# Two more output buffers, an unchecked load of flags and three more branched ranks in a fused attention and mixture-of-experts kernel

## The chip, the cores and the metric

The kernel runs on one core of a Trainium2 chip. The metric is the device time of one execution in microseconds (us). The engines are named as the profile names them: PE is TensorE with its matmuls, PEld its loads of weights, DVE is VectorE, ACT is ScalarE, POOL is GpSimd and SP is SyncE, which here issues most of the transfers.

## The reference, cut to what matters

A clustered attention feeds a mixture of experts. Queries and keys of 4 batches, 8 heads and 768 positions are each assigned to one of 16 centroids, and a query sees only the keys of its own cluster. The result, 3072 rows of 512 numbers, is the input of the experts. Four groups of four experts make 16; every row goes to one expert, found by two argmax (group, then expert in the group), and its result is scaled by the product of the two softmax weights:

```python
for g in range(G):
    mask_g = g_idx == g
    xg = x[mask_g]
    ...
    for e in range(Eg):
        mask_e = e_idx == e
        h = np.maximum(xg[mask_e] @ w1[g, e], 0.0)
        ye = h @ w2[g, e]
        combined = g_w[mask_g][mask_e] * e_w[mask_e]
        out[tok_idx] = combined[:, None] * ye
```

Here `w1` of one expert is 512 x 1024 and `w2` 1024 x 512, in float32. The kernel computes each product in float16 with a high and a low part, so that one product becomes three: high by high, high by low and low by high.

## The kernel before, in words

The attention and the routing take the first 400 us or so. The experts follow, and the change lies there alone. The expert with most rows is treated first, in a part A and a part B that is woven into it (`bridge`). The other fifteen are sorted by their number of rows, and the sorted place is the rank. Rank k has a fixed capacity, `caps` at line 773: 288, 272, 256, 240, 232, 224, 216, 208, 200, 192, 184, 176, 168, 160 and 160 rows. One round of the loop in `ranks` holds the first product of rank k (`up`) and the second product of rank k - 1 (`down`), eight steps of each, taken in turn, and between them the next pieces of the stream of weights (`fill`): a load by SP, the high part by ACT or POOL (line 833 or 835), the low part by DVE (line 836).

The order of the instructions on PE, ACT and DVE is the order of the program (`manual_schedule` with PINNED, line 1511). An instruction that waits therefore holds all that stands behind it on its engine. POOL and SP are not pinned in that list, but work in the order of their queues as well.

`up` (line 1047) computes two of eight feature blocks at a time, each in a psum tile out of three. ACT takes the relu out of each into `hh` (line 1069) and DVE the low part into `hl` (line 1070); after that the psum tile is free again. `down` (line 1074) has two ways. Rank 2 goes by rows: the result is an output tile of up to 128 rows at once. The other ranks go by features (`feature_major`): four feature blocks of 24 products each, taken out by ACT and DVE into `yh` and `yl` (lines 1104 and 1105), and in the next round `settle` turns them back with PE into output tiles, at step 2.

`emit` (line 1160) finishes an output tile: ACT scales it by the weights of the rows into `y` (line 1163), a tile of 128 x 512 float32 out of three buffers, and POOL issues an indirect transfer that stores the rows where they belong (line 1164). A buffer can be written again when its store has landed.

Most ranks have fewer rows than their capacity. `widths` (line 1274) computes for all ranks at once whether the number of rows is no more than a narrower size, the capacity less an entry of `LESS` (16 for rank 9, 24 for ranks 10 and 11), and packs the answers as bits of one integer, `wi`. PE loads it into a register once, in step 5 of the second half of `bridge` (line 1457). The load has bounds, 0 and 2 to the 16th less one, and these are checked on PE at run time. `at_width` (line 1297) then writes a block of products twice, under an `If` and its `Else`, with the narrow or with the full number of columns; a block's first product, which starts the sum, is full in both. All blocks of `up` branch so, 12 products for each of two feature blocks. Those of `down` do for ranks under `CHOSEN`, 9 (line 761), in one group of 24 products; from rank 9 on a feature block is two groups of 12 products without a branch, one at an even and one at an odd step.

The tile `xTA` (line 940) has 4 x 2 x 256 float16 numbers on each partition. It holds the turned rows of part A and is read by the first products of part A.

Of the kernel before, what the change touches and what calls it, by code (L numbers as in the profile page):

```python
# [14 lines left out]
F32 = mybir.dt.float32  # L15
# [4 lines left out]
ET = mybir.EngineType  # L20
# [4 lines left out]
P = 128  # L25
# [720 lines left out]
class Experts:  # L746
# [11 lines left out]
    TURNED, TURN = (3, 4, 6, 14), 3  # L758
    HI = (0, 0, 0, 1, 0, 0, 0, 1)
    LEAD = 12  # L760
    CHOSEN, BOUND = 9, 15
    LESS = 16, 32, 32, 24, 24, 24, 24, 24, 24, 16, 24, 24, 24, 16, 24

    def __init__(self, ctx, tc, R, w1, w2, out, stage, wa):
# [137 lines left out]
    def fetch(self):  # L902

        nc, R, CA, KD = self.nc, self.R, self.CA, self.R.KD
        nt = -(-CA // P)
        sz = [min(P, CA - t * P) for t in range(nt)]
        tab = self.small("tabA", [P, nt, 2])
        tv = R.table.rearrange("(e s) w -> e s w", s=R.BS)[bass.ds(self.f0, 1)].rearrange("e s w -> (e s) w")
        self.nt = -(-max(self.caps) // P)
        self.tb = self.small("tb", [R.E, self.nt * P, 2])  # L910
        while R.done < R.B - 2:
            yield
        for _ in range(READ + 2):
            yield
        with self.after(), self.tc.issue_after(self.cfg["mr"].ins) if "mr" in self.cfg else ExitStack():
            for t, n in enumerate(sz):
                R.reads(nc.sync.dma_start(out=tab[0:n, t], in_=tv[t * P:t * P + n]))
            R.reads(nc.sync.dma_start(out=self.tb, in_=R.table.rearrange("(e s) w -> e s w", s=R.BS)[0:R.E, 0:self.nt * P]))
        for _ in range(READ):
            yield  # L920
        ids = self.small("idA", [P, nt], I32)
        g = self.small("gA", [P, nt])
        with self.after():
            for t, n in enumerate(sz):
                nc.vector.tensor_copy(out=ids[0:n, t:t + 1], in_=tab[0:n, t, 0:1])
                nc.vector.tensor_scalar(out=g[0:n, t:t + 1], in0=tab[0:n, t, 1:2], scalar1=1.0 / (XS * WS * WS), scalar2=None, op0=ALU.mult)
        self.colsA = [g[0:n, t:t + 1] for t, n in enumerate(sz)], [ids[0:n, t:t + 1] for t, n in enumerate(sz)]

        rows = R.N - R.N // R.B
        xgs = []  # L930
        for t, n in enumerate(sz):
            xf = self.cfg["ld"].tile([P, KD * P * 3 // 2], F32, name=("qx", "kx", "vx")[t])[:, 0:self.D]
            nc.vector.memset(xf, 0.0)
            xgs.append(xf.bitcast(F16).rearrange("p (k a x) -> p k a x", a=2, x=P))
            if rows:
                with self.tc.issue_after(self.cfg["los"][0].ins) if "los" in self.cfg else ExitStack():
                    self.gather(ids[0:n, t:t + 1], n, xgs[t], rows)
            for _ in range(2):
                yield
        xTA = self.wa.tile([P, KD, 2, CA], F16, name="xTA")  # L940
        self.xTA = xTA.rearrange("p k a m -> p a k m")
        for t, n in enumerate(sz):
            nc.sync.dma_start_transpose(out=xTA.rearrange("p k a m -> p (k a) m")[:, :, t * P:t * P + n], in_=xgs[t][0:n].rearrange("p k a x -> p (k a x)"))
            yield

    def open(self, ctx):
        tc = self.tc
        late = ctx.enter_context(tc.tile_pool(name="econst2", bufs=1))
        self.small = lambda name, shape, dt=F32: late.tile(shape, dt, name=name)
        self.stage2 = ctx.enter_context(tc.tile_pool(name="stage2", bufs=2))  # L950
        wp = ctx.enter_context(tc.tile_pool(name="wp", bufs=1))
        self.W = [[self.wtiles(wp, 0, n) for n in "ab"], [self.WA[2:4], self.wtiles(wp, 1, "b")]]
        self.xp = ctx.enter_context(tc.tile_pool(name="mxp", bufs=2))
        self.pinned, self.left, self.widen = False, None, False
        self.owed, self.wrote, self.again = [], [], False
        self.back = late.tile([P, P], F16, name="back")
        self.nc.vector.tensor_scalar(out=self.back, in0=self.cfg["ident"], scalar1=YS, scalar2=None, op0=ALU.mult)
        self.ps_y = ctx.enter_context(tc.tile_pool(name="ps_y", bufs=2, space=PSUM))
# [200 lines left out]

    def emit(self, py, n, g, idc):  # L1160
        nc = self.nc
        y = self.xp.tile([P, self.D], F32, name="y", bufs=3)
        nc.scalar.activation(out=y[0:n], in_=py[0:n, 0:self.D], func=AF.Copy, scale=g)  # L1163
        d = self.put = nc.gpsimd.indirect_dma_start(  # L1164
            out=self.out, out_offset=bass.IndirectOffsetOnAxis(ap=idc, axis=0),
            in_=y[0:n], in_offset=None, bounds_check=self.R.N - 1, oob_is_err=False)
        if self.again:
            self.R.behind(d, self.wrote)
        else:

            self.R.alone(d, "wrote", self.wrote)
# [263 lines left out]
    def bridge(self, ga, new):  # L1435

        for i in range(8):
            next(ga)
            with self.tc.issue_after(self.mm.ins):
                if i >= self.ADD:  # L1440
                    next(new, None)
        self.pinned = True
        with self.tc.manual_schedule(engines=PINNED):
            h = []
            up = None
            for i in range(8):
                next(ga)
                if self.left:
                    self.left()
                    self.left = None  # L1450
                for _ in range((2, 1, 0, 1)[i] if i < 4 else 0):
                    next(new, None)
                if i == 0:
                    self.xTB = self.tokens_b()
                    up = self.up(self.xTB, self.CB, self.WA[0:2], h)
                if i == 5:
                    self.word = self.nc.values_load(self.wi[0:1, 0:1], engines=[ET.PE], min_val=0, max_val=2 ** self.R.E - 1)
                for _ in range(self.BESIDE[i]):
                    next(up)
                if i == self.SLOTS:  # L1460
                    self.slots()
                if i >= self.SLOTS:
                    next(self.fill)
            for _ in ga:
                pass
            xT = self.tokens(self.xg0, self.caps[0])
            for _ in up:
                next(self.fill)
            self.settle()
        return xT, self.xg0, None, self.down(h, self.CB, self.WA[2:4], [self.gB], [self.idB])  # L1470
# [238 lines left out]
```

## Time and profile before

| | |
|---|---|
| Timed runs, median of three | 713.98 us (713.72 to 715.66) |
| Profiled execution | 716.25 us |
| Its span, first to last instruction | 714.4 us |
| Around the span | 1.85 us |
| Mean granted clock of TensorE, as a share | 0.992 |

The profile is one execution. The busy time of an engine says how much of the span it worked, not whether the end waited for it. For that there is the chain of waits, which is followed back from the last instruction, at each step to what released it. A timeline row gives the start and the length of one or more instructions of a line, with the tiles written and read (out<-in), their shape, and in brackets the idle time of the engine before it and what ended that. Rows whose engine ends in q are the sequencer's: it handles loads of registers, branches and waits and hands the rest on to the engine's queue. The ends of matmuls are modelled, so the distance between matmuls is read from their starts.

### The profile page before, as it was taken

The numbers are of one execution on the slowest core, as the hardware profiler recorded it, in microseconds if no ns is written. First come the engines' busy times: TensorE is split into PE (matmuls) and PEld (weight loads), VectorE is DVE, ScalarE is ACT, GpSimd is POOL, SyncE is SP. The second block draws the span as 40 slices with busy tenths as digits, with TensorE's granted clock in tenths as the row PEclk, the third lists the DMA queues.
The fourth block names the chain that finished last, engine by engine and source line by source line (L and its number), as shares of the span: only waits on it lengthen the run. The fifth ranks groups of instructions, "written<-read, shape, count | busy, mean of one in ns | idle before, by whom it ended". The sixth has DMA issues, their size and how long they took to land.

```text
span 714.4 us, 25953 instructions
## 1 busy us (share of the span) xinstructions
PE 683.5 (96%) x10528; PEld 585.7 (82%) x10528; DVE 581.4 (81%) x1226; ACT 500.5 (70%) x948; POOL 459.4 (64%) x522
## 2 busy tenths in 40 slices
PE   5989999999999999999999989999899999999996
PEld 3667887887788887887778857898599999999995
DVE  5998989899798998989887836768488788888961
ACT  5558898897888978977996336665446666667642
POOL 9768888899988999989985032324524254453442
PEclk9999999999999999999999999999999999999998
DMA  8765737557486474552755179899789899888721
GB/s 254 201 176 158 201 89 189 136 125 196 96 167 157 110 203 100 116 120 52 167 119 106 61 265 313 283 353 226 279 257 293 272 289 302 300 286 294 217 78 48
DMA packets 89528, 136.74 MB, mean 191 GB/s; under 512 B 41508, under 2 KB 59428, under 8 KB 89385
## 3 DMA queue, kind: packets, MB, share of 16 engines
q1 hardware_dynamic: 83884, 121.32, 61.0%
q0 software_dynamic: 5344, 13.38, 5.6%
q8 instruction: 102, 1.67, 1.0%
q14 instruction: 42, 0.34, 0.2%
q10 hardware_dynamic: 156, 0.03, 0.0%
HBM read 93.17 MB, written 13.99 MB: 150 GB/s over the span
## 4 chain that ended last, share of the span: by engine, by line
PE 64%; DVE 14%; ACT 9%; DMA 6%; issue 5%; POOL 1%; SPq 1%; POOLq 0%; ACTq 0%; DVEq 0%
PE psh L1064 15%; PE psy L1098 14%; PE pso L395 10%; PE psc L320 6%; PE psf L362 5%; PE psf L363 5%; DVE mpart L323 5%; ACT p L367 3%; PE psy L1122 2%; PE psm L253 2%; DMA xT<-xg 1%; PE psm L1150 1%; PE psm L1032 1%; DMA vx<-vr 1%; DMA out_dram<-y,ri 1%
## 5 line engine op out<-in xcount | busy, mean ns | idle before, releaser
L374 POOL TENSOR_TENSOR pl<-p 128x512 f16<-128x512 f32 x193 | 198.8, 1055 | 20.3 <-ACT p L367 19.1
L323 DVE TENSOR_REDUCE mpart<-psc 128x1 f32<-128x512 f32 (+1 forms) x282 | 188.4, 681 | 17.8 <-PE psc L320 16.0
L367 ACT ACTIVATE p<-psf 128x512 f32<-128x512 f32 x288 | 171.8, 599 | 41.5 <-PE psf L363 33.6
L395 PE MATMUL pso<-V,pl 128*128 128x65 f16 (+1 forms) x1968 | 161.0, 193 | 0.0
L362 PE MATMUL psf<-A 82*128 82x384 f16 (+2 forms) x576 | 143.9, 274 | 2.3 <-ACT p L367 0.8
L363 PE MATMUL psf<-B 128*128 128x384 f16 (+2 forms) x576 | 143.7, 274 | 0.0
L395 PEld LDWEIGHTS <-pl 128*128 128x128 f16 x1968 | 130.9, 97 | 1.8 <-issue 0.4
L395 PEld LDWEIGHTS <-p 128*128 128x128 bf16 x1632 | 112.4, 98 | 20.3 <-issue 0.5
L395 PE MATMUL pso<-V,p 128*128 128x65 f16 x1632 | 120.8, 193 | 0.0
L374 POOL TENSOR_TENSOR pl<-p,ph 128x512 f16<-128x512 f32 x84 | 96.8, 1161 | 24.8 <-POOL pl L374 9.6
L320 PE MATMUL psc<-A 80*128 80x512 f16 (+1 forms) x376 | 107.6, 331 | 4.4 <-DVE mpart L323 3.0
L1069 ACT ACTIVATE hh<-psh 128x256 f16<-128x256 f32 (+14 forms) x136 | 46.1, 346 | 79.6 <-PE psh L1064 61.6
L1022 POOL DMA_INDIRECT xg<-xbuf,ri x32 | 35.1, 1098 | 84.2 <-PE psm L1032 38.4
L1070 DVE SCALAR_TENSOR_TENSOR hl<-psh,hh 128x256 f16<-128x256 f32 (+14 forms) x136 | 47.0, 365 | 36.3 <-ACT hh L1069 34.1
L1064 PE MATMUL psh<-xT,wh0a 128*128 128x272 f16 (+14 forms) x512 | 66.0, 246 | 3.2 <-DVE hl L1070 3.0
L363 PEld LDWEIGHTS <-B 128*128 128x128 f16 x576 | 56.8, 99 | 13.5 <-issue 4.1
L362 PEld LDWEIGHTS <-A 82*128 82x128 f16 x576 | 56.0, 98 | 10.3 <-issue 1.8
L1064 PE MATMUL psh<-xT,wl0a 128*128 128x272 f16 (+7 forms) x256 | 59.5, 245 | 0.0
L1064 PE MATMUL psh<-xT,wh0b 128*128 128x272 f16 (+6 forms) x448 | 57.2, 245 | 0.1
L1164 POOL DMA_INDIRECT out_dram<-y,ri x32 | 40.2, 1256 | 22.1 <-ACT y L1163 14.9
L371 ACT CAST ph<-p 128x512 f16<-128x512 f32 x84 | 51.9, 617 | 2.3
L1064 PE MATMUL psh<-xT,wl0b 128*128 128x240 f16 (+6 forms) x224 | 52.3, 244 | 0.0
(328 smaller groups left out, 1607.8 us busy)
## 6 DMA issues: line engine op xcount, KB each, us to landing
st<-w SPq DMA_DIRECT2D x88, 512.0 KB
B<-parts SPq DMA_DIRECT2D x64, 192.0 KB
wh<-w SPq DMA_DIRECT2D x21, 512.0 KB
wl<-w SPq DMA_DIRECT2D x19, 512.0 KB
kx<-kT SPq DMA_DIRECT2D x16, 384.0 KB
qx<-qT SPq DMA_DIRECT2D x16, 384.0 KB
vx<-vr SPq DMA_DIRECT2D x16, 384.0 KB
A<-parts SPq DMA_DIRECT2D x32, 192.0 KB
```

The costliest lines, as they stand in the source:

```text
L320: last["mm"] = nc.tensor.matmul(out=pc[:, off:off + k1 - k0], lhsT=QA[h % 8][0:80, c * P:(c + 1) * P], rhs=KA[h % 8][0:80, k0:k1], start=T ...
L323: nc.vector.tensor_reduce(out=(mp[:, 0, 0:1], mp[:, :, 1], mp[:, 1, 0:1])[i], in_=pc.rearrange("p (a x) -> p a x", a=n), axis=AX.X, op=ALU ...
L362: nc.tensor.matmul(out=o, lhsT=KA[h % 8][0:82, ks], rhs=QA[h % 8][0:82, q0:q1], start=True, stop=False)
L363: nc.tensor.matmul(out=o, lhsT=KBs[h][:, ks], rhs=QBs[h][:, q0:q1], start=False, stop=True)
L367: cfg["exp"] = nc.scalar.activation(out=p32, in_=pf, func=AF.Exp, scale=QK / (SQ * SQ))
L371: nc.scalar.copy(out=ph, in_=p32)
L374: lo = (nc.vector if u in (EARLY if h < 2 else DVE_LO[h % 8] if h < NH - 2 else DVE_END[h - NH]) else nc.gpsimd).tensor_tensor(out=pl, in0 ...
L395: nc.tensor.matmul(out=O[:, col:col + v.shape[-1]], lhsT=p[:, bs], rhs=v, start=c == 0 and q == 0 and i == 0, stop=c == NCH - 1 and i == l ...
L1064: self.mm = nc.tensor.matmul(out=ph[:, 0:n], lhsT=w[:, k, f * P:(f + 1) * P], rhs=xT[:, a, k, 0:n], start=i == 0, stop=i == 3 * KD - 1)
L1069: nc.scalar.activation(out=hh[:, f], in_=ph[:, 0:M], func=AF.Relu)
L1070: self.ev = nc.vector.scalar_tensor_tensor(out=hl[:, f], in0=ph[:, 0:M], scalar=0.0, in1=hh[:, f], op0=ALU.max, op1=ALU.subtract)
L1098: self.mm = nc.tensor.matmul(out=py[:, 0:n], lhsT=w[:, f, d * P:(d + 1) * P], rhs=a[:, f, 0:n], start=i == 0, stop=i == len(prods) - 1)
```

## The change

Three things change. `CHOSEN` goes from 9 to 12, so that the second products of ranks 9, 10 and 11 stand under a branch on the flag of their rank, in one group of 24. The load of the flags is told to skip the check at run time. And `emit` counts the output tiles: where the loop stands at rank 1 or later (`widen`), two of every five tiles are written not to one of the three buffers but to the two halves of `xTA`, seen as float32. `again` holds only in a part of the program that does over what did not fit, which this data does not need.

```diff
-    CHOSEN, BOUND = 9, 15
+    CHOSEN, BOUND = 12, 15
...
         xTA = self.wa.tile([P, KD, 2, CA], F16, name="xTA")
         self.xTA = xTA.rearrange("p k a m -> p a k m")
+        self.yown = xTA.rearrange("p k a m -> p (k a m)").bitcast(F32)[:, 0:2 * self.D].rearrange("p (t d) -> p t d", d=self.D)
...
-        self.pinned, self.left, self.widen = False, None, False
+        self.pinned, self.left, self.widen, self.ny = False, None, False, 0
...
     def emit(self, py, n, g, idc):
         nc = self.nc
-        y = self.xp.tile([P, self.D], F32, name="y", bufs=3)
+        self.ny += 1
+        if self.widen and not self.again and self.ny % 5 < 2:
+            y = self.yown[:, self.ny % 5]
+        else:
+            y = self.xp.tile([P, self.D], F32, name="y", bufs=3)
...
-                    self.word = self.nc.values_load(self.wi[0:1, 0:1], engines=[ET.PE], min_val=0, max_val=2 ** self.R.E - 1)
+                    self.word = self.nc.values_load(self.wi[0:1, 0:1], engines=[ET.PE], min_val=0, max_val=2 ** self.R.E - 1, skip_runtime_bounds_check_because="a sum of distinct powers of two below 2 ** E")
```

## Rows read from the trace of the kernel before

**Rows 1.** The page: busy us, share, instructions by engine; queue: packets, MB, share
```profile
PE 683.5 (96%) x10528; PEld 585.7 (82%) x10528; DVE 581.4 (81%) x1226; ACT 500.5 (70%) x948; POOL 459.4 (64%) x522
...
q8 instruction: 102, 1.67, 1.0%
```

**Rows 2.** Busy time by window: length, each engine's us, clock, DMA share, GB/s
```profile
640.00:660.00 20.00, 20.00 (x287) 19.86 (x286) 17.84 (x28) 14.01 (x29) 7.78 (x8) 1.00 0.91 307
```

**Rows 3.** The chain of waits, 500 to 530 us: start, us, what
```profile
505.22 7.39 DMA out_dram<-y,ri
...
514.35 1.50 DVE wl0b L836
...
517.76 0.41 DVE hl L1070
```

**Rows 4.** Timeline of ACT, 470 to 482 and 498 to 526 us
```profile
480.11 1.82 ACT L1163 ACTIVATE y<-psm,rg 128x512 f32<-128x512 f32 x3
...
502.15 1.82 ACT L1163 ACTIVATE y<-psm,rg 128x512 f32<-128x512 f32 x3 [1.42 <-PE psm L1150]
...
512.69 0.69 ACT L1163 ACTIVATE y<-psy,rg 128x512 f32<-128x512 f32 x1 [5.58 <-DMA out_dram<-y,ri]
```

**Rows 5.** Timeline of PE, 518 to 532 us
```profile
518.21 0.36 PE L1064 MATMUL psh<-xT,wh0a 128*128 128x232 f16 x2 [3.01 <-DVE hl L1070]
...
519.39 1.67 PE L1098 MATMUL psy<-hh,wh 128*128 128x240 f16 x8
...
523.19 0.35 PE L1064 MATMUL psh<-xT,wh0a 128*128 128x232 f16 x2
...
525.35 0.91 PE L1098 MATMUL psy<-hh,wh 128*128 128x240 f16 x8
...
527.58 0.35 PE L1064 MATMUL psh<-xT,wh0a 128*128 128x232 f16 x2
```

**Rows 6.** Busy time by window, 519.2 to 523.2 us
```profile
519.20:523.20 4.00, 4.00 (x28) 3.45 (x27) 4.00 (x6) 2.25 (x3) 0.00 (x0) 0.57 0.88 282
```

**Rows 7.** The chain of waits, 400 to 440 us
```profile
420.14 0.55 PE psh L1064 x12
420.69 1.29 PE psy L1122 x6
...
425.01 1.10 issue
...
426.36 1.77 PE psy L1122 x6
```

**Rows 8.** Line 1457: operation, count, ns min/median/max, first and last start
```profile
L1457 PEldq SEQ_ASSERT  x1: 28/28/28, 419.7 to 419.7; - x1
```

**Rows 9.** Groups by line and form, PE, 624 to 640.3 us: busy us, mean ns
```profile
L1064 PE MATMUL psh<-xT,wh0a 128*128 128x160 f16 x56 | 6.8, 233 | 0.0
```

**Rows 10.** Timeline of PE, second products of ranks 9 and 13
```profile
625.70 0.82 PE L1098 MATMUL psy<-hh,wh 128*128 128x192 f16 x8
626.36 0.82 PE L1098 MATMUL psy<-hh,wl 128*128 128x192 f16 x8
...
686.60 0.72 PE L1098 MATMUL psy<-hh,wh 128*128 128x160 f16 x8
687.15 0.72 PE L1098 MATMUL psy<-hh,wl 128*128 128x160 f16 x8
```

**Rows 11.** Line 1304, the branches
```profile
L1304 PEldq COMPARE_BRANCH  x184: 65/132/1628, 431.5 to 696.5; - x184
```

**Rows 12.** Line 1098, second products: PE idle before them, us, times
```profile
  issue: 0.3, 1
```

**Rows 13.** Line 1584, a second load into a register of PE
```profile
L1584 PEldq TENSOR_LOAD <-anyi x1: 319/319/319, 597.9 to 597.9; - x1
```

**Rows 14.** Timeline of SP, 457 to 480 us
```profile
473.12 0.74 SPq L826 DMA_DIRECT2D wh<-w  x1
```

**Rows 15.** Timeline of ACT, 470 to 482 us
```profile
475.15 1.05 ACT L833 ACTIVATE wh0b<-wh 128x1024 f16<-128x1024 f32 x1
```

## The prediction

> **What bounds the kernel now.** I read the page first: the tensor engine (PE) is busy 96% of the span, the vector engine (DVE) 81%, the scalar engine (ACT) 70% [rows 1]. The busy time by windows says the same of the part that is changed: from 640 to 660 us PE is busy 20.00 of 20 us at full clock, DVE 17.84 [rows 2]. So in the ranks a microsecond saved on PE is a microsecond of the end, unless DVE or a transfer takes its place, and a stall of any other engine counts only where it reaches PE. I therefore looked for the places where PE stands still after 400 us. There are two.
>
> The first is in the chain of waits around 505 to 518 us [rows 3]. The reader is to see it begin with a store, `out_dram<-y`, that takes 7.39 us from issue to landing, and go on through ACT and a DVE operation of the weights to `hl`, and only then to PE. The timeline of ACT tells what the store holds [rows 4]: three outputs `y` are written from 502.15, and the next one starts at 512.69, after 5.58 us of waiting for `out_dram<-y`. Three buffers, so the tenth output takes the buffer of the seventh, whose store left at 505.22 and landed about 512.6. ACT works in order; behind that `y` stand the relus `hh` of the next pair of products, behind them DVE's `hl`, and behind `hl` the three psum tiles of `up`. PE's timeline shows the price [rows 5]: the products at 518.21 start after 3.01 us of idle time that `hl` ended. After it PE runs slow: 24 second products take from 519.39 to 523.19, 3.80 us, where the same 24 take from 525.35 to 527.58, 2.23 us. [...] Together 4.6 us.
>
> The second is in the chain at 422 to 428 us [rows 7]. Twelve products of 104 columns take 0.55 us at 420.14; the next twelve should start at 421.98 (420.69 + 1.29) and the chain reaches the work behind them only at 426.36, with pieces named "issue" between, the longest 1.10 us. That loses 4.38 - 0.55 = 3.8 us, and the six products behind take 1.77 us instead of 1.29: 4.3 us in all, with a little more behind. Nothing that the profile shows releases it. What came shortly before on PE's own queue is the load of the flags, line 1457, and the check of its bounds, a SEQ_ASSERT at 419.7 us, the only one on PE [rows 8].
>
> **The change part by part.** The sum is made against the profiled execution: 716.25 us, of them 714.4 span and 1.85 around it. The median of the three timed runs is 713.98, 2.3 us lower; I take the savings over to it unchanged.
>
> *Two more buffers.* Five buffers in turn instead of three: the tenth output takes the place of the fifth, which was written in the group from 480.11 [rows 4], 27 us before it is wanted again. The wait of 5.58 us goes, ACT writes `y` near 507 and keeps its order, and PE's 3.0 us and the slow clock behind it go with it: 4.6 us. No other `y` waits for a store in the timeline, and from rank 2 on there are only two outputs a rank, so nothing else is won. What is late next at that place: the DVE operation of the weights at 514.35, behind which `hl` could start only at 517.76, 3.4 us later [rows 3]. It would run some 5 us earlier, when PE's three psum tiles are not yet all full; were it late all the same, up to 3.4 us of the gain stay away. The store itself adds nothing: the same stores leave from the same queue. The lower end is nothing gained, or a loss by a wait inside the new memory (a rival below). The buffers lie in `xTA`, which is last read in part A, before the ranks, so the first use waits for nothing.
>
> *The second products of ranks 9 to 11 branch.* The flags of these ranks are set in this data: the first products of rank 10 run at 160 columns, not 184 [rows 9]; the same view shows 176 instead of 192 for rank 9 and 152 instead of 176 for rank 11 (three groups in all). The pitch of the second products is read from starts: eight of 192 columns take from 625.70 to 626.36, 82.5 ns each; eight of 160 from 686.60 to 687.15, 68.8 ns each [rows 10]. That is 0.43 ns a column. In each of four feature blocks 23 of 24 products get narrower (the first stays wide), so 92 a rank: 92 x 0.43 x (16 + 24 + 24) columns = 2.5 us. All of it is on PE, and PE is full there [rows 2]. Against it stand 12 more branches. The branch instructions of line 1304 take 65 to 1628 ns, 132 in the median, 184 of them [rows 11], but they stand in the sequencer, ahead of PE's queue: the 32 branched blocks of second products left PE idle once, for 0.3 us [rows 12]. So 12 x 0.3 / 32 = 0.1 us; the bounds are 0 and twelve of the longest; I take 0.2 for the odd long one. The order changes a little: 12 products that stood before the settling of an older rank now stand behind it, as they do for ranks 0 to 8, where PE does not wait for it. DVE has 17.84 us of work in 20 [rows 2]; were even 1.5 us of such a stretch saved, it would have 17.84 of 18.5. That still fits; I count 0, with 0.5 us as the far end.
>
> [...]
>
> *The flags without a check.* The instructions of the check go, the last of them 28 ns long [rows 8]. While they ran, PE had products queued and went on without a gap until 421.98 [rows 7], so by themselves they cost 0. The open question is whether they cause the trickle that follows 2.2 us later. For it: it is the only such stall of PE after 400 us and stands behind the only check on PE. Against it: eighteen products behind the check, at 420.14 and 420.69, still came in pace, and the loading itself stays. The second load on PE, line 1584 at 597.9 us, has no check on PE and is followed by no such trickle [rows 13]; that speaks against the load and so a little for the check. Bounds 0 and 4.3 us; I take 0, because the check is done and those eighteen products are through before anything is late.
>
> Sum: 716.25 - 4.6 - 2.5 + 0.2 = 709.35 us for the profiled execution, 713.98 - 6.9 = 707.1 us for the median.
>
> **The rivals.**
> 1. *The check was the stall.* Then 4.3 us come on top: 707.1 - 4.3 = 702.8, and somewhat less with what runs slow behind it. For and against as above. Chance 0.30.
> 2. *The buffer's wait is replaced.* ACT passes `y`, but DVE, late beside POOL, or ACT's weights hold `hl` at the same place, and PE idles as long. Then the narrow products alone count: 713.98 - 2.3 = 711.7. Against it: before 507 us neither engine has a backlog in the chain; all of it there grows behind `y`. Chance 0.10.
> 3. *The new pair is taken as one tile: slower.* Both new buffers are halves of one tile. If a write to the second half waits for the store that reads the first, then wherever outputs 5 and 6, 20 and 21, 30 and 31 follow each other in one settling, ACT waits as it did at 512.69, and PE loses 4.6 us each time (10 and 11 are a half round apart): 713.98 - 6.9 + 3 x 4.6 = 720.9. It turns the sign from two such waits on. Against it: SP loads into `wh` at 473.12 [rows 14] while ACT still reads a part of `wh` at 475.15 [rows 15], so halves of one tile do move apart here. Chance 0.07.
> 4. *The branches eat what the narrow products give.* A block that is jumped over is 24 products and 24 weight loads. The page counts 23,752 instructions on the engines and 1.67 MB of them fetched, so at most 70 bytes each, in packets of 16.4 KB [rows 1]: 3.4 KB a block, so about 12 x 3.4 / 16.4 = 2.5 of the jumps cross into another packet; if each shows on PE for the longest branch of 1.63 us, 4.0 us are lost instead of 0.2: 707.1 + 3.8 = 710.9. [...] Chance 0.08.
>
> **How the numbers follow.** My forecast, buffers and columns, has 0.42 and a range of its own of 705 to 709.5 (part of the 3.4 us and 0.5 of DVE left, or a part of the second stall won). The rivals have 0.30, 0.10, 0.07 and 0.08; 0.03 is left for no change. The likeliest is 707.1. The range that leaves out no more than 2 in 10 runs from 701.0 (rival 1 and a little more) to 711.8 (rival 2). A measurement of this kernel tells about 0.3%, 2.1 us, from no change, so rival 2 lies on that border and half of it counts as the same: faster 0.85, same 0.08, slower 0.07.
>
> **What would show it.** Right: no `y` of ACT that waits for `out_dram`; PE without idle time between 510 and 520 us and no stretch of lower clock there; second products of 176, 160 and 152 columns in ranks 9 to 11, and each of these rounds 0.6 to 0.95 us shorter, PE still at 20 of 20. The forecast is too high if the pieces of "issue" after line 1457 are gone, and the weights of rank 0 start some 4 us earlier. It is wrong if ACT waits for the store at outputs 6, 21 or 31, if PE idles at the same place for DVE, or if PE shows gaps behind the twelve new branches.

## The result and the profile after

| | before | changed |
|---|---|---|
| Median of six runs each | 714.82 us (712.79 to 716.15) | 707.26 us (705.67 to 709.83) |
| Profiled execution, its span | 716.25 us, 714.4 us | 706.70 us, 704.9 us |
| Ratio, 95% interval | | 0.9896 (0.9872 to 0.992) |

Three of the six runs of before are those shown ahead of the prediction. The time fell 7.6 us, and the forecast was 707.1. That agreement says little of the reasons: one step was right, one had the wrong sign, and part of the difference is most likely not the change's. The traces show it. Ratios here leave out the runs over 1.5% above the fastest of their kernel and are not the quotients of the medians beside them; where the two differ and it matters, both are given.

**The buffers.** ACT's timeline of the changed kernel (start, length, what was written from what, idle time before it):

```profile
499.65 0.68 ACT L1168 ACTIVATE xTA<-psy,rg 128x512 f32<-128x512 f32 x1
...
506.86 0.69 ACT L1168 ACTIVATE xTA<-psy,rg 128x512 f32<-128x512 f32 x1 [1.32 <-issue]
```

The output that waited 5.58 us for a store [rows 4] is now the one at 499.65, which goes into `xTA` and waits for none. PE's timeline at the place of [rows 5], every row without idle time before it:

```profile
508.77 0.91 PE L1099 MATMUL psy<-hh,wh 128*128 128x240 f16 x8
...
511.00 0.35 PE L1065 MATMUL psh<-xT,wh0a 128*128 128x232 f16 x2
...
513.16 0.91 PE L1099 MATMUL psy<-hh,wh 128*128 128x240 f16 x8
...
515.39 0.35 PE L1065 MATMUL psh<-xT,wh0a 128*128 128x232 f16 x2
```

The 24 second products take 2.23 us from the first time on (508.77 to 511.00), where they took 3.80 and then 2.23. The windows (columns as in [rows 2]) answer to [rows 6] with full clock, and to [rows 2] with a surprise:

```profile
510.00:514.00 4.00, 4.00 (x46) 4.00 (x44) 2.99 (x5) 2.57 (x6) 0.39 (x1) 1.00 0.77 264
...
640.00:660.00 20.00, 17.71 (x274) 16.84 (x272) 16.98 (x26) 11.55 (x24) 6.38 (x7) 1.00 0.78 262
```

**The branches.** Of the 20 us from 640 on, PE now stands for 2.3, at full clock. The chain of waits there shows for what (start, us, what):

```profile
609.78 0.31 PE psy L1099 x4
610.09 0.51 issue
610.60 1.69 PE psy L1099 x20
...
613.97 1.84 PE psy L1099 x24
615.81 0.90 issue
...
639.13 1.67 PE psy L1099 x24
640.80 1.33 issue
642.12 0.92 PE psm L1033 x16
...
646.43 0.62 issue
```

The products are narrower, as forecast: 24 of them take 1.84 and 1.67 us. But behind them stand pieces in which PE waits for nothing that the views name. Behind the longest of them PE's sequencer was in a branch. These are the branches that start between 614 and 615 us and between 639.3 and 639.5 us, then all branches in the part of the changed ranks (columns as in [rows 11]: count, ns min/median/max, starts):

```profile
L1309 PEldq COMPARE_BRANCH  x1: 2225/2225/2225, 614.3 to 614.3; - x1
...
L1309 PEldq COMPARE_BRANCH  x1: 2654/2654/2654, 639.4 to 639.4; - x1
...
L1309 PEldq COMPARE_BRANCH  x46: 73/126/2654, 606.8 to 655.1; - x46
```

The branch from 639.4 to 642.1 us ends where PE's gap ends, at 642.12. Six branches of these ranks last 0.9 to 2.7 us (at 614.3, 619.8, 629.9, 639.4, 650.6 and 655.1). The line of the second products, which was left idle once for 0.3 us [rows 12], and the page's row of fetched instructions, 102 packets before [rows 1], in the changed kernel:

```profile
  issue: 2.1, 5
```

```profile
q8 instruction: 105, 1.72, 1.0%
```

**The trickle.** The chain at the place of [rows 7]:

```profile
418.14 1.29 PE psy L1123 x6
419.44 0.55 PE psh L1065 x12
419.99 1.29 PE psy L1123 x6
421.28 0.56 PE psh L1065 x12
```

The pieces of "issue" are gone, just as rival 1 would have it. They were nevertheless not the check's, as the experiments show. These pieces are called the trickle below, since PE's products arrive there in ones and twos.

**The account.** Both kernels run the same number of products on PE, so the n-th product of one trace can be set against the n-th of the other. Start in the changed kernel less start in the kernel before, in us; the second column takes the profiled execution shown above, the third another of the same kernel (e12_before, below), which had no trickle:

| at, us of the kernel before | against the first profile | against e12_before |
|---|---|---|
| 420 | -2.55 | -0.95 |
| 433 | -7.34 | -0.95 |
| 505 | -7.34 | -0.96 |
| 530 | -12.19 | -8.09 |
| 606 | -12.58 | -8.11 |
| 665 | -9.06 | -5.67 |
| last product | -9.41 | -5.90 |

So the buffers give 4.85 us in the one (7.34 to 12.19) and 7.1 in the other, the ranks that branch now lose 3.5 or 2.4, and 7.3 us of the second column were there by 433 us: 2.55 of scatter in the identical part before the ranks, and 4.8 of trickle.

### The profile page after: what moved, and what is told of

It reads as the page before. It is cut to its first block, busy times and chain, and to the rows that moved or that the text cites. A ratio compares the mean times of both kernels' runs of the same rounds, so it can differ in the third digit from the quotient of the medians.

```text
span 704.9 us, 25971 instructions
## 1 busy us (share of the span) xinstructions
PE 676.2 (96%) x10528; PEld 580.3 (82%) x10528; DVE 582.7 (83%) x1226; ACT 501.7 (71%) x948; POOL 459.6 (65%) x522
## 4 chain that ended last, share of the span: by engine, by line
PE 71%; DVE 13%; ACT 8%; issue 4%; DMA 1%; POOL 1%; POOLq 0%; DVEq 0%; SPq 0%; ACTq 0%
PE psh L1065 17%; PE psy L1099 15%; PE pso L395 11%; PE psc L320 6%; PE psf L362 6%; PE psf L363 6%; DVE mpart L323 5%; PE psy L1123 4%; ACT p L367 3%; PE psm L1151 2%; PE psm L253 2%; PE psm L1033 1%; PE psm L633 1%; ACT psm L853 1%; ACT ph L371 1%
## 5 line engine op out<-in xcount | busy, mean ns | idle before, releaser
L1023 POOL DMA_INDIRECT xg<-xbuf,ri x32 | 37.7, 1178 | 74.4 <-PE psm L1033 32.0
L320 PEld LDWEIGHTS <-A 80*128 80x128 f16 x384 | 37.7, 100 | 15.5 <-issue 5.6
```

The source lines that it names most:

```text
L320: last["mm"] = nc.tensor.matmul(out=pc[:, off:off + k1 - k0], lhsT=QA[h % 8][0:80, c * P:(c + 1) * P], rhs=KA[h % 8][0:80, k0:k1], start=T ...
```

## The experiments

The experiments stand in four groups, e1 to e4, e5 to e8, e9 to e11 and e12, each on a chip of its own, with runs of the kernel before beside it that the group shares. Single runs of a kernel spread by 3 to 14 us, so a ratio has an interval of some 0.3 to 0.5% to either side.

**e1_buffers**: the kernel before with the buffers alone.

```diff
+        self.yown = xTA.rearrange("p k a m -> p (k a m)").bitcast(F32)[:, 0:2 * self.D].rearrange("p (t d) -> p t d", d=self.D)
...
-        y = self.xp.tile([P, self.D], F32, name="y", bufs=3)
+        self.ny += 1
+        if self.widen and not self.again and self.ny % 5 < 2:
+            y = self.yown[:, self.ny % 5]
+        else:
+            y = self.xp.tile([P, self.D], F32, name="y", bufs=3)
```

> The kernel before with the two more buffers alone. Theory A, read from the two traces (each part has its own effect: buffers -4.6, check -4.7, branches +3): 4.6 us faster than before, about 0.9935, no y that waits for out_dram and no stretch of lower clock near 520 us, but the pieces of issue at 422 to 426 us still there. Rival B, the forecast (buffers -4.6, check 0, branches -2.3) says the same of this run. Rival C (the stall near 515 us only moves to DVE or the weights): within 1 us of before.

Measured: 705.43 us (702.58 to 707.63) beside 711.97 of before; ratio 0.9938 (0.9902 to 0.9973), so 4.4 us less (1.9 to 7.0); the quotient of the medians is 0.9908, 6.5 us. In its trace no output waits for a store, PE doesn't stand near 515 us, and there is no trickle, though the check is there. One gap of PE is left in the ranks, and its row names a weight tile (PE's timeline):

```profile
546.36 0.33 PE L1065 MATMUL psh<-xT,wh0a 128*128 128x216 f16 x2 [0.65 <-DMA st<-w]
```

The tile can't be the whole cause. PE's sequencer was in a branch from 543.97 to 545.78 us there, and e4 and e7 have the same gap, 0.58 and 0.38 us, behind the same branch (1.74 and 1.54 us), with the tile there in time.

**e2_unchecked**: the kernel before with the load of the flags unchecked, nothing else.

```diff
-... min_val=0, max_val=2 ** self.R.E - 1)
+... min_val=0, max_val=2 ** self.R.E - 1, skip_runtime_bounds_check_because="a sum of distinct powers of two below 2 ** E")
```

> The kernel before with the load of the flags unchecked and nothing else. Theory A: 4 to 5 us faster than before (ratio about 0.9935), twelve products of 104 columns in about 0.55 us each time from 418 to 430 us, no issue pieces there, the stall near 515 us unchanged. Rival B: 0 us, the issue pieces stay where they are.

Measured: 712.65 us (706.41 to 717.77); ratio 1.0008 (0.9968 to 1.0049). Nothing is won. Without the buffers the stall is there, and larger than in the first profile; ACT's and then PE's timeline:

```profile
507.77 0.69 ACT L1163 ACTIVATE y<-psy,rg 128x512 f32<-128x512 f32 x1 [8.63 <-DMA out_dram<-y,ri]
...
513.28 0.55 PE L1064 MATMUL psh<-xT,wh0a 128*128 128x232 f16 x2 [6.05 <-DVE hl L1070]
```

**e3_branches**: the kernel before with the twelve branches alone.

```diff
-    CHOSEN, BOUND = 9, 15
+    CHOSEN, BOUND = 12, 15
```

> The kernel before with CHOSEN 12 and nothing else. Theory A: 0 to 3 us slower than before (up to 1.0045); PE idles 3 to 6 us in all behind branches of 1 to 2.6 us in the rounds of ranks 10 to 12, against 2.5 us that the narrower products give. Rival B: 2.3 us faster (0.9968), no gaps of PE in these rounds.

Measured: 716.2 us (706.68 to 721.19); ratio 1.0045 (0.9999 to 1.0091): slower, by an interval that ends at no change. With less work for PE it takes 3 us more, not 2.3 less. Its profile, of its longest execution, has seven branches of 1.4 to 2.8 us from 626 us on and pieces of "issue" up to 1.83 us behind them.

**e4_buf_unchecked**: the changed kernel without the twelve branches.

```diff
-    CHOSEN, BOUND = 12, 15
+    CHOSEN, BOUND = 9, 15
```

> The changed kernel with CHOSEN back at 9: buffers and unchecked load. Theory A: about 9.3 us faster than before (0.987) and 2 to 3 us faster than the changed kernel, no idle time of PE in the rounds of ranks 10 to 12. Rival B: 4.6 us faster than before (0.9935), 2.3 us slower than the changed kernel.

Measured: 705.14 us (704.1 to 707.42); ratio 0.9939 (0.9905 to 0.9973). That is e1 again (0.9938): the check adds nothing beside the buffers either. No gap of PE over 0.12 us after 606 us.

The second group takes the branch edit apart: **e5_changed** is the changed kernel again, **e6_buf_unchecked2** is e4 again.

> The changed kernel once more, beside the next three on one chip. Theory A (the twelve new branches cost PE 3 to 5 us of idle time, the narrower products give 2.5): 1 to 3 us slower than the kernel with buffers and unchecked load alone (e6). Rival B (the slower runs of the branches alone were scatter between executions; branches cost 0.2): 2.3 us faster than e6.

> Buffers and unchecked load with CHOSEN 9, again, as the base for e5, e7 and e8 on one chip. Both theories: about 0.994 of before.

**e7_narrow_unbranched**: the changed kernel with narrow second products in ranks 9 to 11 and no branch around them. It leaves out the full width that these ranks need with other data.

```diff
-                    self.at_width(rank if two else None, M, products)
+                    if two and rank > 8:
+                        products(self.narrow(rank))
+                    else:
+                        self.at_width(rank if two else None, M, products)
```

> The changed kernel with the second products of ranks 9 to 11 always at the narrow width, in one group of 24 and without a branch (it leaves out the full width for these three ranks, which this data does not use). Theory A and rival B: 2.5 us faster than e6. Theory A: 4 to 5 us faster than e5, no long idle time of PE in the rounds of ranks 10 to 12. Rival B: within 0.3 us of e5.

**e8_branch_full**: the changed kernel with its twelve branches, but both ways at full width.

```diff
-                    self.at_width(rank if two else None, M, products)
+                    self.at_width(rank if two else None, M, products, two and rank > 8)
...
-            body(self.narrow(k))
+            body(M if full else self.narrow(k))
```

> The changed kernel with both ways of the new branches at full width for ranks 9 to 11: the branch without its gain. Theory A: 2 to 5 us slower than e6, with branches of 1 to 2.7 us and PE idle behind them; wider products in the queue cover a little more than in e5. Rival B: 0.2 us slower than e6.

Measured, beside 711.32 of before:

| | median, us | ratio (95%) | 600 to 665 us, against e6, trace |
|---|---|---|---|
| e6: full width, no branch | 706.11 | 0.9943 (0.991 to 0.9975) | 0 |
| e7: narrow, no branch | 702.82 | 0.9882 (0.9839 to 0.9926) | -2.1 us |
| e8: full width, branch | 707.49 | 0.9944 (0.9916 to 0.9972) | +1.4 us |
| e5: narrow, branch | 707.19 | 0.9965 (0.9934 to 0.9995) | +2.8 us |

The last column sets n-th product against n-th product as above: e5 and e6 run within 0.06 us of each other from 150 to 530 us, e5 is 0.21 us ahead at 606, then it falls back to +2.56 us by 665. For the first profile of the changed kernel the same column gives +3.2, and for e4, which is the program of e6 again, +0.3: so far apart are two executions of one program there. So the narrow products are worth 2.1 us by the traces and 3.3 by the medians (4.3 by the ratios); with a branch around them that turns into a loss. PE's busy time in the stretch (columns as in [rows 2]) and the branches there (as in [rows 11]), first two rows of e6, then two of e5, the changed kernel:

```profile
606.00:656.00 50.00, 50.00 (x714) 49.44 (x712) 43.67 (x70) 33.58 (x68) 23.47 (x23) 1.00 0.88 299
```

```profile
L1309 PEldq COMPARE_BRANCH  x28: 73/126/312, 606.7 to 655.7; - x28
```

```profile
606.00:656.00 50.00, 45.88 (x666) 44.30 (x665) 42.99 (x66) 32.70 (x67) 20.66 (x22) 1.00 0.87 285
```

```profile
L1309 PEldq COMPARE_BRANCH  x48: 73/126/2876, 606.5 to 656.0; - x48
```

In 50 us e6 has no gap, and no branch over 0.31 us; e5 has 4.1 us of gaps and branches up to 2.88 us. The six long branches stand at the places of the first profile: 613.4, 619.5, 629.1, 639.1, 649.6 and 654.2 us. e8, with the same branches around wider products, has long branches too, three of the six among them and up to 1.59 us, and little of them reaches PE (the same two views):

```profile
606.00:656.00 50.00, 49.44 (x692) 48.35 (x690) 43.01 (x68) 34.72 (x68) 22.45 (x24) 1.00 0.88 291
```

```profile
L1309 PEldq COMPARE_BRANCH  x49: 73/176/1587, 606.4 to 655.1; - x49
```

**e9_shifted**: the changed kernel with 32 products of one column (64 PE instructions) put behind the warm-up, so that all later code of PE lies elsewhere.

```diff
+    w = ps_o.tile([P, 512], F32, name="pso")
+    for _ in range(32):
+        nc.tensor.matmul(out=w[:, 0:1], lhsT=wz[:, 0:P], rhs=wz[:, 0:1], start=True, stop=True)
```

> The changed kernel with 32 products of one column (64 instructions of PE, a quarter of a fetched packet) put behind the warm-up at the start; they may cost up to 1 us there. Theory A2 (a branch is long where its jump ends in a packet that is not fetched yet, so it goes by the place of the code): the long branches of the changed kernel, the same six in both of its profiles (about 614, 619.5, 629.5, 639, 650 and 655 us), are short here and others of the 24 in ranks 10 to 12 are long instead. Rival D (a branch is long when the transfers are crowded, so it goes by the time): the same six stay long.

**e10_before** and **e11_before**: the kernel before, two more profiles on e9's chip.

> The kernel before, unchanged, a second profile. Theory A3 (the trickle behind the check was an accident of the one execution profiled, the wait for the store is there in most executions with a length that varies): no issue pieces at 422 to 426 us, an idle time of PE of 0 to 7 us near 515 us that hl ends. Rival E (the trickle belongs to the kernel with the check): the issue pieces are there again.

> The kernel before, a third profile; as for e10, and the idle time of PE near 515 us differs from that of e10 by more than 1 us.

Measured: e9 715.08 us (712.2 to 718.6) beside 721.57 of before on this slower chip; ratio 0.9951 (0.991 to 0.9993), not told apart from e5's. The long branches moved with the code: 1.0 to 1.5 us at 604.3, 640.9, 655.9 and 665.6 us, fewer than in e5, but PE still has 3.8 us of gaps between 611 and 661, not all behind a branch in the records. Where the code lies changes which jumps are long; that it can make them free is not shown. e8, with the same code, has three of the six short, so the time counts as well. More telling is the other stall. e9 loads its flags without a check, and here is its PE at 422 us:

```profile
422.37 0.25 PE L1068 MATMUL psh<-xT,wh 128*128 128x104 f16 x2 [0.78 <-issue]
423.11 0.38 PE L1126 MATMUL psy<-wh,hh 128*128 128x512 f16 x1 [0.44 <-issue]
425.32 0.26 PE L1068 MATMUL psh<-xT,wh 128*128 128x104 f16 x2 [0.38 <-issue]
```

The trickle without the check. e10 (722.14 us) has one piece of it, 0.57 us, e11 (718.11 us) has three, up to 1.07 us. The stall for `hl` is in both, 5.87 and 4.10 us, with a granted clock of 0.50 behind it in e10.

**e12_before**: the kernel before once more.

> The kernel before, a fourth profile. The pieces of issue near 422 to 426 us (4.8 us) were in three profiles of this kernel and in one of a kernel without the check, and in none of nine others, two of them with the check. Theory that they belong to the chip or the hour: if the times of this chip lie near 711 us, no such pieces, PE goes on from one group of twelve products to the next in 1.8 us, and the time is near 711; if they lie near 718 to 722, pieces of 0.4 to 1.1 us again. Theory that they belong to this very program (its instructions and where they lie): pieces of 2 to 4 us in sum whatever the chip. Both expect PE to stand 3 to 6.6 us for hl near 515, behind an output that waits for a store.

Measured: 708.02 us (704.67 to 714.01) beside 706.37 of the same kernel; the profiled execution took 714.01. The chain of waits at the trickle's place, then ACT's and PE's timelines at the stall's:

```profile
420.39 0.55 PE psh L1064 x12
420.94 1.29 PE psy L1122 x6
422.23 0.56 PE psh L1064 x12
```

```profile
508.50 0.69 ACT L1163 ACTIVATE y<-psy,rg 128x512 f32<-128x512 f32 x1 [7.79 <-DMA out_dram<-y,ri]
...
514.01 0.55 PE L1064 MATMUL psh<-xT,wh0a 128*128 128x232 f16 x2 [5.21 <-DVE hl L1070]
```

The same program, check and all, without a trickle. Of fourteen profiles, all three from e9's chip have it, and the first of before; the ten others have none: those of e1 to e8 and e12, from three chips, and the first of the changed kernel. So it goes with the chip or the hour and not with the kernel.

**What the long branches wait for.** Each trace records every DMA packet, with those of the instruction queue q8, of 16 KB each. Set beside the six long branches of the changed kernel (first profile, us):

| branch starts | packet of q8 lands | branch ends | PE goes on after a gap |
|---|---|---|---|
| 614.29 | 615.08 | 616.51 | 616.71 |
| 619.77 | 619.98 | 621.41 | 621.60 |
| 629.90 | 629.61 | 630.97 | no gap |
| 639.41 | 640.57 | 642.06 | 642.12 |
| 650.58 | 650.70 | 652.12 | 652.18 |
| 655.08 | 654.52 | 655.96 | no gap |

Each ends 1.36 to 1.50 us after a landing. The fourteen traces hold 106 branches of PE of 0.5 us or more, and every one ends 1.21 to 1.62 us after the latest packet of q8 landed. For the 2340 branches of up to 0.25 us that time is anything from 0 to 14 us. So, by these landings, the long branches wait for instructions. Straight code does too: the 0.51 us of "issue" before 610.60 stand four products into a group of 24 and end 1.34 us after a landing, and e9's gaps of 1.06 and 1.03 us, which end at 617.58 and 653.10, end 1.40 and 1.52 us after one, with no long branch ahead. During the trickle no packet of q8 is on its way in any of the four profiles that have it, so the trickle is something else.

## Why the prediction came out as it did

*Two more buffers: right.* Forecast 4.6 us by the removal of the wait (3.01 us of PE) and of the slow clock behind it (1.57 us, which is 3.80 less 2.23, at a granted clock of 0.57 [rows 6]). The step came as written: no `y` waits for `out_dram`, PE runs through, the clock stays full (1.00 from 510 to 514 us). e1 puts it at 4.4 us (6.5 by the medians), the traces at 4.85 and 7.1. The wait is not a constant: six profiles without the buffers have PE standing 3.01, 4.10, 5.21, 5.87, 6.05 and 6.58 us there, so the 3.0 of the first profile was the shortest of them. None of the eight profiles with the buffers has it. Neither DVE's weights (rival 2) nor the pair in one tile (rival 3) took its place.

*The flags without a check: right, at 0.* e2 alone is 1.0008, e4 and e1 are equal, and the trickle comes without the check (e9) and stays away with it (e1, e3, e12). Rival 1, which had a chance of 0.30, falls, although the first profile after looks like its proof: the trickle was in the one execution and not in the other. What causes it stays open.

*The second products: the narrow columns right, the branches wrong.* The pitch came as forecast (eight products of 160 columns from 639.53 to 640.08 us, 68.8 ns each), and 92 products a rank at fewer columns are worth 2.1 us (traces, e7 against e6) to 3.3 (medians), beside 2.5 in the sum. The step that failed is "So 12 x 0.3 / 32 = 0.1 us; the bounds are 0 and twelve of the longest; I take 0.2 for the odd long one." With narrow products the branches cost 4.4 us by the medians (707.19 less 702.82) and 4.9 by the traces (2.8 + 2.1), so the edit costs 1.1 us by the medians and 2.8 by the traces where 2.3 were to be won. The intervals of e5 and e7 don't overlap. The error was to carry over an idle time from 32 blocks at earlier ranks in one execution. Other executions have more idle time there: near 541 to 552 us e1, e2, e4 and e7 lose 0.38 to 0.78 us behind one branch. And the cover was larger there: 24 second products take 2.23 us near 510 us, and 1.84, 1.67 and 1.6 us here, less than the longest branches (2.65 us in the first profile of the changed kernel, 2.88 in e5). e8 shows the same with the width alone changed, 1.4 us lost at full width against 4.9.

The outcome is rival 4's, which had 0.08. Its 4.0 us were close to the 4.4 to 4.9 measured, but by luck: it had 2.5 jumps that cost 1.63 us each, and the trace has seven gaps of 0.18 to 1.33 us, 4.2 us in all, two of them inside a group of products. It would have put the kernel at 710.9; e5's ratio applied to the 713.98 that the forecast started from gives 711.5. What the traces show of the cause: six of the branches here last 0.9 to 2.7 us where the median is 0.13, each ends 1.36 to 1.50 us after a packet of instructions landed, and e9 shows that the long ones move with the code. That a jump is long where it crosses into another packet was the author's estimate; no run shows which jumps cross, and the gaps inside groups of products are no case of a branch.

*The sum.* 707.26 against 707.1 most likely because two misses cancel. The edit of the branches came out 3.4 to 5.1 us slower than the sum had it. The other way, the first comparison holds 7.6 us, while the changed kernel beside before on one chip gives 0.9965 (2.5 us; 4.1 by the medians), and e9, with its 64 extra instructions, 0.9951 (3.5 us; 6.5 by the medians). The trickle of 4.8 us in the first profile of before is of the size of that difference, and a longer wait for the store would do it too (7.1 us in e12 against 4.85). Which of them the timed runs of before had isn't shown, since only profiled executions have a trace. The chance of 0.85 for faster by over 0.3% holds on the first pair; by the ratio of e5 the gain is about 0.35%, on that border.

*A better version.* e4 and e6, the change without its twelve branches, took 705.14 and 706.11 us, where before had 711.97 and 711.32 and the changed kernel 707.19. The intervals of e6 and e5 overlap; what tells them apart is the 2.8 us by which their traces part between 600 and 665 us, where two executions of one program part by 0.3 to 0.4.

## What to carry to other kernels

Before blaming a branch, set its end beside the landing of the last packet of instructions (here the end came 1.21 to 1.62 us later for every branch of 0.5 us or more). Price it by the cover at its own place: compare the longest branch of the trace with the time of the products queued ahead of it there (here 2.65 us beside 1.67), and don't average over places with wider products. A stall found in one profile may be an accident until a second profile of the same kernel shows it; the stall at `hl` was in all four profiles of the kernel before, with lengths from 3.0 to 5.9 us, the trickle in three. And when a forecast is met, take the edit apart all the same: here it was met though one of its three steps had the wrong sign.

## What the runs showed of the hardware

- The branches around blocks of 24 products and 24 weight loads took PE's sequencer 0.07 to 2.88 us (e5, 48 of them from 606 to 656 us). Six were long at the same places in two executions of the changed kernel, and others with 64 instructions put ahead.
- All 106 branches of PE of 0.5 us or more in fourteen traces end 1.21 to 1.62 us after a 16 KB packet of instructions landed. Gaps between products with no long branch ahead end so too (1.34, 1.40 and 1.52 us after a landing).
- Two executions of nearly the same program on one chip can stay within 0.06 us of each other from 150 to 530 us (e5 and e6), while runs of one kernel there spread by 3 to 13 us. Two aligned traces can then show a difference of 2 to 3 us that twelve timed runs of each leave open.
- On one chip (e9 to e11) all three profiles had PE's products between 421 and 427 us arrive in ones and twos, with idle pieces of 0.2 to 1.1 us that nothing in the profile ends and no packet of instructions goes with. It was not settled why.
- A store that an output waits for held ACT between 5.58 and 10.07 us in six executions of code that is the same up to there, but for the check that e2 leaves out.
